# Bucketed attention in front of two MLPs: P's products one step closer to the exponentials, with a new start and one early weight less

## The chip, the cores and the metric

The kernel runs on one core of a Trainium2 chip. The metric is the device time of one execution, in microseconds (us). The engines are TensorE (PE), VectorE (DVE), ScalarE (ACT) and GpSimd (POOL); SyncE (SP) only issues transfers here, and ACT issues some too. All engines take their instructions in the order written.

## What is computed

```python
def reference(**kw):
    # q, k, v: (2, 8, 768, 64), proj: (64, 6)
    mask = bucket(q @ proj > 0)[..., :, None] == bucket(k @ proj > 0)[..., None, :]
    s = where(mask, q @ k.T / 8, -1e9)          # (2, 8, 768, 768)
    p = exp(s - max(s)); p = p / (sum(p) + 1e-9)
    x = (p @ v) as 1536 tokens x 512            # 8 heads side by side
    x = (sigmoid(x @ w_gate) * (x @ w_val)) @ w_out       # 512 -> 1536 -> 512
    h = x @ w_in; return (h * cos(h)) @ w_out2            # 512 -> 2048 -> 512
```

A query sees only the keys whose six projection signs equal its own. The MLP weights come as 64-bit floats.

## The kernel before

Every product is made of high and low float32r parts: a value is rounded to a high part, what is left is the low part, and three (or two) matmuls are added up.

**Attention** (lines 227 to 689) goes through 16 heads of six row blocks of 128 queries, NG = 96 steps in all. Step g issues, among others:

- S, `scores(g+2)` (396): four matmuls of a row block against 768 keys, in one of two double banks `s_ps`. The bucket condition sits in extra rows of the operands (q2, k2);
- MIN, `rowmax(g+1)` (409), one reduction on DVE, and EXP, `expo(g)` (418), one activation with row sums on ACT;
- every third step COEF (433): the reciprocals of three row sums on DVE, and on POOL the coefficient of fully masked rows; NRM (450): P scaled on POOL, one row block (128x768) an instruction;
- the products of P, LAG steps behind: `ptrans` (465) transposes three row blocks of P for one block of 128 keys, `phi` (ACT) and `plo` (DVE) split it, `pv` (485) adds two matmuls with v. Ta, the transposes of the even block, is the first in a step to read a new group of three row blocks 3u, 3u+1, 3u+2, in step 3u + LAG - 1; Tb has the odd one;
- FIN (493): at a block's end ACT copies the output of half a head, which SP's queue puts in place. Three steps after the second head of a pair, `fin_sum` (524) adds the halves on POOL (128x768); five steps after, `fin_hi` (ACT) and `fin_lo` (POOL) write the tokens' high and low parts;
- W, `early_weights` (646): in some steps one of the NEARLY early weights is converted from 64 to 32 bits, in two parts, on ACT and DVE.

The next heads are prepared on the side by PREP: an ordered list `todo` by step. For a head whose first step is s1: loads at s1-19 and s1-17, transposes of its halves at s1-12 and s1-10 (their split, two POOL instructions at lines 300 and 303, comes in LATE of the next step), `bits` (six matmuls, 348) at s1-8, and `values` (v split on POOL, 261) at s1-3 for even, s1-1 for odd heads. `fin_sum` and `fin_lo` are appended to the same lists. The order in a step is written out by hand, from step LAG - 1 on:

```python
ORDER = (
    "Tb LOa COEF NRM PVb EXP Ta MIN LATE W HIb PVa PREP S FIN HIa PVaF LOb".split()
)
```

Before that the fill steps issue only "COEF NRM MIN EXP LATE W PREP S". Heads 0 and 1 are prepared ahead of the first step (599 to 634): head 0's pieces are copied between partitions on DVE, POOL and ACT, head 1's by transfers.

**The two MLPs** (692 to 859) follow in a list of items, each of which is some 12 to 24 matmuls of 512 columns; weights are converted and split some items ahead by due times (824 to 839). The first items run between the last steps of attention.

Of the kernel before, what the change touches and what calls it, by code (L numbers as in the profile page):

```python
# [40 lines left out]
def lsh_attention_glu_moe_cos_moe(  # L41
# [30 lines left out]
    NEARLY, NWE = 3, 5  # L72
# [135 lines left out]
    order = sorted(use, key=lambda kk: use[kk] - lead(kk)[0])  # L208
# [18 lines left out]
    def attention():  # L227
        nonlocal done
        parts = None
        with ExitStack() as st:  # L230
# [40 lines left out]
            def trans(hd, half, fast=False):  # L271
                hh = heads.setdefault(hd, {})
                if half == 0:
                    hh["x"] = [
                        prep.tile([P, T, P], F32R, tag=f"x{i}", name=f"x{i}_{hd}", bufs=2)
                        for i in range(2)
                    ]
                    for nm in ("q1", "k1", "q2", "k2"):
                        hh[nm] = prep.tile([P, T, P], F32R, tag=nm, name=f"{nm}_{hd}")
                xh, xl = hh["x"]  # L280
                sl = slice(3 * half, 3 * half + 3)
                pt = ps_t.tile([P, 3, P], F32, tag="t", name=f"pt{hd}{half}")
# [3 lines left out]
                def evac():  # L286
                    if fast:
                        nc.scalar.activation(xh[:, sl, :], pt, AF.Copy, scale=qscale)
                        nc.vector.scalar_tensor_tensor(
                            out=xl[:, sl, :],  # L290
                            in0=pt,
                            scalar=qscale,
                            in1=xh[:, sl, :].bitcast(F32),
                            op0=ALU.mult,
                            op1=ALU.subtract,
                        )
                    else:
                        xf = work.tile([P, 3, P], F32, tag="xf", name=f"xf{hd}{half}", bufs=2)
                        nc.scalar.activation(xf, pt, AF.Copy, scale=qscale)
                        nc.gpsimd.tensor_scalar(  # L300
                            out=xh[:, sl, :], in0=xf, scalar1=1.0, scalar2=1.0, op0=ALU.mult, op1=ALU.mult
                        )
                        nc.gpsimd.tensor_tensor(
                            out=xl[:, sl, :], in0=xf, in1=xh[:, sl, :].bitcast(F32), op=ALU.subtract
                        )
                    lo, hi = slice(0, D), slice(D, P)
                    if hd == 0:

                        for eng, nm, rows, src, part in (
                            (nc.vector, "q1", hi, xl, lo),  # L310
                            (nc.gpsimd, "q1", lo, xh, lo),
                            (nc.gpsimd, "k1", hi, xh, hi),
                            (nc.gpsimd, "k2", slice(32, 64), xl, slice(64, 96)),
                            (nc.gpsimd, "k2", slice(64, 96), xl, slice(96, 128)),
                        ):
                            eng.tensor_scalar(
                                out=hh[nm][rows, sl],
                                in0=src[part, sl].bitcast(F32),
                                scalar1=1.0,
                                scalar2=1.0,  # L320
                                op0=ALU.mult,
                                op1=ALU.mult,
                            )
                        if half == 1:
                            for nm, rows, part in (
                                ("k1", lo, hi),
                                ("q2", slice(32, 64), slice(0, 32)),
                                ("q2", slice(64, 96), slice(32, 64)),
                            ):
                                nc.scalar.copy(hh[nm][rows], xh[part].bitcast(F32))  # L330
                            raw.pop(hd)
                        return
                    if half == 0:
                        return
                    raw.pop(hd)
                    for nm, rows, src, part in (
                        ("q2", slice(32, 96), xh, lo),
                        ("k2", slice(32, 96), xl, hi),
                        ("q1", hi, xl, lo),
                        ("k1", lo, xh, hi),  # L340
                        ("q1", lo, xh, lo),
                        ("k1", hi, xh, hi),
                    ):
                        nc.sync.dma_start(hh[nm][rows].bitcast(F32), src[part].bitcast(F32))

                return evac

            def bits(hd):
                pb = ps_t.tile([P, HS], F32, tag="t", name=f"pb{hd}")
                hh = heads[hd]  # L350
                xh, xl = hh["x"]
                for half in range(2):
                    sl = slice(3 * half, 3 * half + 3)
                    cols = slice(0, P) if half else slice(D, D + P)
                    for n, (i, x) in enumerate(((0, xh), (1, xh), (0, xl))):
                        nc.tensor.matmul(  # L356
                            pb,
                            pw[:, i, cols],
                            x[:, sl, :],
                            start=(half == 0 and n == 0),  # L360
                            stop=(half == 1 and n == 2),
                        )

                def code(out, rows):
                    nc.vector.tensor_scalar(
                        out=out,
                        in0=pb[rows],
                        scalar1=bcode[rows, 1:2],
                        scalar2=bcode[rows, 0:1],
                        op0=ALU.is_gt,  # L370
                        op1=ALU.mult,
                    )

                def evac():
                    parts = [
                        (half, nm, slice(D * half + 32 * i, D * half + 32 * i + 32))
                        for half, i, nm in ((0, 0, "q2"), (0, 1, "k2"), (1, 1, "k2"), (1, 0, "q2"))
                    ]
                    if hd > 0:
                        bf = prep.tile([P, HS], F32R, tag="bf", name=f"bf{hd}", bufs=1)  # L380
                        code(bf, slice(0, P))
                    for half, nm, rows in parts:
                        out = hh[nm][0:32, 3 * half : 3 * half + 3].rearrange("p t s -> p (t s)")
                        if hd == 0:
                            code(out, rows)
                        else:
                            nc.sync.dma_start(out.bitcast(F32), bf[rows].bitcast(F32))

                return evac
# [159 lines left out]
            LAG = 7  # L549

            WL, WC = (72, 74, 76), 82
# [8 lines left out]
            for hd in range(2, NH):  # L560
                s1 = T * hd
                if hd > 2:
                    for nm in "qk":
                        at(max(s1 + LOAD_AT[nm], -2), lambda hd=hd, nm=nm: load(hd, nm))
                if hd % 2 == 0:
                    at(max(s1 + LOAD_AT["v"], -1), lambda hd=hd: load(hd, "v"))
                for half in range(2):
# [5 lines left out]
                    else:  # L573
                        at(2 * half, lambda hd=hd, half=half: trans(hd, half))
                at(max(s1 + BITS_AT, 2), lambda hd=hd: bits(hd))
# [4 lines left out]
            def run_late():  # L580
                while late:
                    late.pop(0)()
# [7 lines left out]
            with tc.manual_schedule(  # L590
# [14 lines left out]
                for g in range(2):  # L605
                    nc.sync.dma_start(pj[D * g : D * g + D, :], proj)
# [13 lines left out]
                evac = [trans(0, half, fast=True) for half in range(2)]  # L620
                for fn in evac:
                    fn()
                evac = [bits(0)]
                evac += [trans(1, half, fast=True) for half in range(2)]
                for fn in evac:
                    fn()
# [4 lines left out]
                scores(0)  # L631
                scores(1)
                rowmax(0)
                late.append(bits(1))
                for g in range(NG + LAG + 2):
# [22 lines left out]
                    def norms():  # L658
                        for n in range(g - 3, NG if g == NG else g - 2):
# [16 lines left out]
                        "NRM": (0 <= g - 3 <= NG - 3, norms),  # L676
# [15 lines left out]
    def moe():  # L692
        with ExitStack() as st:
# [210 lines left out]
```

## Time and profile before

| | us |
|---|---|
| median of 3 runs | 806.71 (806.35 to 808.7) |
| profiled execution | 806.87 |
| its span, first to last instruction | 805.1 |
| PE busy in the span | 791.7 (98%) |
| DVE busy | 510.2 (63%) |
| ACT busy | 468.0 (58%) |
| POOL busy | 325.6 (40%) |

The shares are means over the attention part, some 250 us in which all four engines work, and the MLPs, in which mostly PE does. Matmuls are pipelined, so their lengths overlap, and a busy PE is not one at its peak.

### The profile page before, as it was taken

To read this page: it belongs to the slowest core of one execution; us is meant where nothing else is said; L and a number is where in the kernel's file an instruction comes from. 1 tells how busy PE (TensorE), PEld (TensorE's weight loads), DVE (VectorE), ACT (ScalarE), POOL (GpSimd) and SP (SyncE) were. 2 spreads that over 40 slices of the span, in tenths; PEclk is the share of its full clock that TensorE was granted. 3 is DMA by queue.
4 is the path that set the end of the run, shared out by engine and by line. 5 is a ranking of instruction groups with operands and counts; after the bars stand their busy time and mean duration, and the time that the engine had idled before them with its cause. 6 is when DMAs were issued, how large, how long until landed. Compare 5 with 4: busy or idle time off the path is not lost.

```text
span 805.1 us, 11607 instructions
## 1 busy us (share of the span) xinstructions
PE 791.7 (98%) x3984; PEld 680.0 (84%) x3984; DVE 510.2 (63%) x794; ACT 468.0 (58%) x929; POOL 325.6 (40%) x347
## 2 busy tenths in 40 slices
PE   7999999999999999999999999999999999999998
PEld 5899999999988888888888888888888888878886
DVE  6888888888985443333343266667655666586662
ACT  5898989989996322222222254456666656564442
POOL 5879889988972212111121122221222122222221
PEclk9999999999999999999999999999999999999999
DMA  6766765688513333222221112323223333242312
GB/s 157 189 156 155 171 163 138 153 196 212 137 47 108 105 105 93 92 78 79 79 78 53 53 55 102 106 79 107 90 91 104 105 105 103 62 161 94 105 53 104
DMA packets 70746, 89.03 MB, mean 111 GB/s; under 512 B 30112, under 2 KB 54816, under 8 KB 70688
## 3 DMA queue, kind: packets, MB, share of 16 engines
q1 hardware_dynamic: 67104, 84.96, 37.2%
q10 hardware_dynamic: 3584, 3.34, 1.5%
q8 instruction: 31, 0.51, 0.3%
q14 instruction: 27, 0.22, 0.1%
HBM read 59.77 MB, written 3.15 MB: 78 GB/s over the span
## 4 chain that ended last, share of the span: by engine, by line
PE 93%; DVE 3%; ACT 2%; issue 1%; DMA 0%; POOL 0%; DVEq 0%; ACTq 0%; POOLq 0%
PE a L807 16%; PE ph L718 16%; PE pv L718 12%; PE a L780 12%; PE pg L718 12%; PE t L470 7%; PE o L491 4%; PE o L490 4%; PE s L403 4%; PE s L406 4%; PE pb L356 2%; PE pt L284 1%; ACT p L421 1%; DVE mn L414 1%; DVE pl L480 0%
## 5 line engine op out<-in xcount | busy, mean ns | idle before, releaser
L718 PE MATMUL ph<-xy,ih 128*128 128x512 f32 x384 | 118.1, 389 | 0.0
L123 ACT CAST gh<-g 128x512 fp32r<-128x512 f32 x84 | 52.1, 620 | 109.8 <-PE a L807 44.5
L480 DVE TENSOR_TENSOR pl<-t,ph 128x384 fp32r<-128x384 f32 x192 | 102.5, 553 | 15.1 <-ACT ph L475 13.5
L124 POOL TENSOR_TENSOR zl<-w_z,zh 128x512 fp32r<-128x512 f32 x32 | 41.4, 1295 | 167.7 <-ACT zh L123 167.7
L454 POOL TENSOR_SCALAR p<-p,r,d 128x768 f32<-128x768 f32 x96 | 95.2, 996 | 21.1 <-PE s L406 7.7
L744 DVE TENSOR_TENSOR g<-pv,sg 128x512 f32<-128x512 f32 x36 | 24.9, 692 | 123.9 <-PE pv L718 122.6
L475 ACT CAST ph<-t 128x384 fp32r<-128x384 f32 x192 | 90.5, 486 | 17.4 <-PE t L470 15.7
L414 DVE TENSOR_REDUCE mn<-s 128x1 f32<-128x770 f32 x96 | 91.2, 951 | 13.6 <-PE s L406 10.6
L470 PE MATMUL t<-ident,p 128*128 128x128 f32 x576 | 94.4, 272 | 0.0
L124 DVE TENSOR_TENSOR gl<-g,gh 128x512 fp32r<-128x512 f32 x84 | 57.8, 688 | 52.7 <-ACT gh L123 50.5
L421 ACT ACTIVATE p<-s,mn 128x768 f32<-128x768 f32 x96 | 88.1, 918 | 5.1 <-DVE mn L414 4.9
L742 ACT ACTIVATE sg<-pg 128x512 f32<-128x512 f32 x36 | 21.3, 592 | 119.4 <-PE pg L718 119.4
L718 PE MATMUL pg<-xy,gh 128*128 128x512 f32 x288 | 89.3, 390 | 0.0
L718 PE MATMUL pv<-xy,vh 128*128 128x512 f32 x288 | 88.7, 389 | 0.0
L718 PEld LDWEIGHTS ph<-xy,ih 128*128 128x128 f32 x384 | 72.0, 188 | 14.9
L470 PEld LDWEIGHTS t<-ident,p 128*128 128x128 f32 x576 | 74.7, 140 | 7.5
L490 PE MATMUL o<-ph,vs 128*128 128x384 f32 x192 | 79.0, 412 | 0.3 <-ACT e L500 0.3
L807 PE MATMUL a<-zh,gh 128*128 128x512 f32 x192 | 74.8, 390 | 0.2 <-DVE o L817 0.2
L807 PE MATMUL a<-zl,gh 128*128 128x512 f32 x192 | 74.8, 390 | 0.2 <-POOL zl L124 0.2
L807 PE MATMUL a<-zh,gl 128*128 128x512 f32 x192 | 74.8, 390 | 0.0
L718 PE MATMUL ph<-xy,il 128*128 128x512 f32 x192 | 74.7, 389 | 0.0
L403 PE MATMUL s<-k,q 96*128 96x384 f32 x192 | 69.7, 363 | 2.1 <-ACT p L421 2.1
(105 smaller groups left out, 1748.3 us busy)
## 6 DMA issues: line engine op xcount, KB each, us to landing
raw_z<-in_moe_w_out SPq DMA_DIRECT2D x32, 512.0 KB, 3.3
raw_o<-in_moe_w_out SPq DMA_DIRECT2D x23, 512.0 KB, 3.3
q<-x SPq DMA_DIRECT2D x45, 192.0 KB, 3.1
k<-x SPq DMA_DIRECT2D x45, 192.0 KB, 3.5
raw_i<-in_moe_w_in SPq DMA_DIRECT2D x16, 512.0 KB, 3.9
raw_v<-in_moe_w_val SPq DMA_DIRECT2D x10, 512.0 KB, 3.5
raw_g<-in_moe_w_gate SPq DMA_DIRECT2D x9, 512.0 KB, 3.7
nv<-in_v SPq DMA_DIRECT2D x8, 384.0 KB, 4.5
```

The lines of the kernel that those rows point to most:

```text
L124: sub.tensor_tensor(out=dst_l, in0=src, in1=dst_h.bitcast(F32), op=ALU.subtract)
L403: nc.tensor.matmul(o, hh["q2"][0:96, t, :], hh["k2"][0:96, sl, :], start=True, stop=False)
L414: nc.vector.tensor_reduce(mn_t[u][:, i : i + 1], s_t[g][:, :, 0 : HS + 1], axis=AX.XY, op=ALU.min)
L421: nc.scalar.activation(pt, s_t.pop(g)[:, :, 0:HS], AF.Exp, bias=mn_t[u][:, i : i + 1], scale=-1.0, accum_out=sm_t[u][:, i : i + 1],)
L454: nc.gpsimd.tensor_scalar(out=pt, in0=pt, scalar1=r[:, i : i + 1], scalar2=d[:, i : i + 1], op0=ALU.mult, op1=ALU.add,)
L470: nc.tensor.transpose(pt[:, i, :], pv_[:, j * P : (j + 1) * P], ident)
L475: nc.scalar.copy(ph, pt_t[w])
L480: nc.vector.tensor_tensor(out=pl, in0=pt_t.pop(w), in1=ph_t[w].bitcast(F32), op=ALU.subtract)
L490: nc.tensor.matmul(o_t[u], vs[:, j, :], ph_t.pop(w), start=(j == 0), stop=False)
L718: nc.tensor.matmul(ps, w[:, kt, :], xy[c][:, hl, kt, :], start=(n == 0), stop=(n == 11))
L780: nc.tensor.matmul(acc[c, e], w[:, e, :], m, start=(f == 0 and n == 0), stop=(f == F1 - 1 and n == 2),)
L807: nc.tensor.matmul(acc[c, t], m[:, ts], w, start=(f == 0 and n == 0), stop=(f == F2 - 1 and n == 2),)
```

## The change

1. LAG goes from 7 to 6. The norms of a group, one in each of the steps 3u+3, 3u+4 and 3u+5, become two in step 3u+3 and one in 3u+4.
2. Two weights instead of three are converted during attention (NEARLY), from step 84 instead of 82; no conversion is made at the MLPs' item 0; the first output weight goes ahead of the second value weight.
3. Head 0 is prepared in an order written by hand (`first_head`): the bits of its two halves go to two banks, k's part and q's first block are coded first. The first scores and the first minimum come ahead of head 1's low parts. Head 1's loads are issued ahead of the bucket constants.
4. Head 2 is split from PSUM by ACT and DVE (as head 1 was) instead of by POOL, one step apart. For every head the high-part matmuls of `bits` come ahead of the low-part ones, and the six transfers that place a head's parts have another order.

```diff
-    NEARLY, NWE = 3, 5
+    NEARLY, NWE = 2, 5
-    order = sorted(use, key=lambda kk: use[kk] - lead(kk)[0])
+    order = sorted(use, key=lambda kk: use[kk] - lead(kk)[0] - 1.5 * (kk == ("o", 0, 0)))
...
+                for low in range(2):
+                    for half in range(2):
+                        for i in range(2 - low):
+                            nc.tensor.matmul(
+                                pb,
+                                pw[:, i, slice(0, P) if half else slice(D, D + P)],
+                                hh["x"][low][:, 3 * half : 3 * half + 3, :],
...
+            def first_head():
+                split = [trans(0, half, fast=True) for half in range(2)]
...
+                pb = [s_ps[1][0:D, 0, 0:HS], ps_o.tile([P, HS], F32, tag="o", name="pb0")[0:D]]
...
+                for high, _ in split:
+                    high()
+                for _, low in split:
+                    low()
                 for half in range(2):
...
+                for ts in (h0, h1):
+                    move(nc.gpsimd, "k1", hi, ts, xh, hi)
+                    for part in (64, 96):
+                        move(nc.gpsimd, "k2", slice(part - 32, part), ts, xl, slice(part, part + 32))
+                move(nc.scalar, "k1", lo, every, xh, hi)
+                move(nc.scalar, "q1", lo, h0, xh, lo)
+                for part in (0, 32):
+                    move(nc.scalar, "q2", slice(part + 32, part + 64), h0, xh, slice(part, part + 32))
+                move(nc.vector, "q1", hi, h0, xl, lo)
+                k_code(0)
+                q_code(0, 0, 1)
+                k_code(1)
+                q_code(0, 1, 3)
+                q_code(1, 0, 3)
+                move(nc.gpsimd, "q1", lo, h1, xh, lo)
+                move(nc.gpsimd, "q1", hi, h1, xl, lo)
...
-            LAG = 7
+            LAG = 6
-            WL, WC = (72, 74, 76), 82
+            WL, WC = (72, 74, 76), 84
...
-                        at(max(s1 + LOAD_AT[nm], -2), lambda hd=hd, nm=nm: load(hd, nm))
+                        at(max(s1 + LOAD_AT[nm], -2) if hd > 3 else 2, lambda hd=hd, nm=nm: load(hd, nm))
...
-                at(max(s1 + BITS_AT, 2), lambda hd=hd: bits(hd))
+                at(s1 + BITS_AT if hd > 2 else 5, lambda hd=hd: bits(hd))
...
-                    nc.sync.dma_start(pj[D * g : D * g + D, :], proj)
+                    (nc.sync, nc.scalar)[g].dma_start(pj[D * g : D * g + D, :], proj)
+                load(1, "k")
+                load(1, "q")
                 for g in range(2):
                     nc.sync.dma_start(
                         bcode[D * g : D * g + D],
...
-                load(1, "q")
-                load(1, "k")
-                load(0, "v")
                 load(2, "k")
                 load(2, "q")
+                load(0, "v")
                 bit_weights()
...
+                rest = first_head()
+                split = [trans(1, half, fast=True) for half in range(2)]
+                for high, _ in split:
+                    high()
+                place(1, 0)
+                rest()
+                scores(0)
+                scores(1)
+                rowmax(0)
...
+                late.append(first_low)
+                at(1, lambda: bits(1)())
                 values(0)
                 values(1)
...
-                        for n in range(g - 3, NG if g == NG else g - 2):
+                        for n in {0: range(g - 3, NG if g == NG else g - 1), 1: (g - 2,), 2: ()}[g % 3]:
                             norm(n)
...
-                        "NRM": (0 <= g - 3 <= NG - 3, norms),
+                        "NRM": (3 <= g <= NG, norms),
...
-                    convert_at[k] = max(early, k - NEARLY, split_at[order[k - NWE]] if k >= NWE else 0)
+                    convert_at[k] = max(early, k - NEARLY, 1, split_at[order[k - NWE]] if k >= NWE else 0)
```

## Rows read from the trace of the kernel before

**Rows 1.** The page, busy time and share of each engine
```profile
PE 791.7 (98%) x3984; PEld 680.0 (84%) x3984; DVE 510.2 (63%) x794; ACT 468.0 (58%) x929; POOL 325.6 (40%) x347
```

**Rows 2.** Windows: stretch, length, busy us (instructions) by engine, clock, DMA share
```profile
3.80:13.60 9.80, 8.96 (x29) 7.31 (x30) 8.23 (x16) 5.38 (x8) 7.04 (x12) 1.00 0.62 147
16.20:17.60 1.40, 0.29 (x4) 0.06 (x2) 1.17 (x2) 1.03 (x3) 1.22 (x2) 1.00 1.00 232
17.60:24.30 6.70, 5.44 (x29) 4.38 (x29) 4.14 (x7) 4.93 (x12) 4.93 (x7) 1.00 0.87 195
60.00:200.00 140.00, 140.00 (x941) 133.00 (x941) 121.06 (x205) 128.63 (x306) 125.01 (x153) 1.00 0.69 168
```

**Rows 3.** Timeline of PE, steps 46 to 48; start us, length us, engine, operation
```profile
117.73 1.29 PE L356 MATMUL pb<-x,pw 128*128 128x384 f32 x6
...
120.59 0.49 PE L470 MATMUL t<-ident,p 128*128 128x128 f32 x3
...
122.66 0.61 PE L470 MATMUL t<-ident,p 128*128 128x128 f32 x3
```

**Rows 4.** Timeline of POOL, steps 45 to 47
```profile
114.99 0.98 POOL L454 TENSOR_SCALAR p<-p,r,d 128x768 f32<-128x768 f32 x1 [1.10 <-PE s L406]
115.95 0.51 POOL L300 TENSOR_SCALAR x<-xf 128x384 fp32r<-128x384 f32 x1
...
117.53 0.50 POOL L265 TENSOR_SCALAR vs<-nv 128x384 fp32r<-128x384 f32 x1
...
119.11 0.99 POOL L454 TENSOR_SCALAR p<-p,r,d 128x768 f32<-128x768 f32 x1
120.06 1.85 POOL L527 TENSOR_TENSOR ef<-e,ef 128x768 f32<-128x768 f32 x1
121.88 1.00 POOL L454 TENSOR_SCALAR p<-p,r,d 128x768 f32<-128x768 f32 x1
```

**Rows 5.** Timelines of ACT and DVE, steps 43 and 45
```profile
111.21 0.49 ACT L500 COPY e<-o 128x384 f32<-128x384 f32 x1
...
114.63 0.17 DVE L447 RECIPROCAL r<-sm 128x3 f32<-128x3 f32 x1
```

**Rows 6.** Line 527, the sum: nanoseconds least, median, most; first and last start
```profile
L527 POOL TENSOR_TENSOR ef<-e,ef x8: 1017/1836/1851, 62.9 to 246.4; 128x768 f32<-128x768 f32 x7, 128x384 f32<-128x384 f32 x1
```

**Rows 7.** Timelines of POOL and PE, steps 10 and 11
```profile
34.00 1.95 POOL L454 TENSOR_SCALAR p<-p,r,d 128x768 f32<-128x768 f32 x2
...
35.14 0.49 PE L470 MATMUL t<-ident,p 128*128 128x128 f32 x3
```

**Rows 8.** Timelines of DVE and POOL, step 83
```profile
207.14 1.22 DVE L160 SCALAR_TENSOR_TENSOR w_g<-wp_g,wl_g 128x512 int32<-128x512 int32 x1
...
207.80 1.41 POOL L454 TENSOR_SCALAR p<-p,r,d 128x768 f32<-128x768 f32 x1
```

**Rows 9.** Timelines of SyncE's queue, DVE, ACT and PE, the start
```profile
4.91 0.65 SPq L256 DMA_DIRECT2D nqk<-in_k  x1
...
8.19 0.66 DVE L365 TENSOR_SCALAR q<-pb,bcode 32x384 fp32r<-32x384 f32 x1 [0.26 <-PE pb L356]
...
10.99 1.14 DVE L289 SCALAR_TENSOR_TENSOR x<-pt,qscale,x 128x384 fp32r<-128x384 f32 x2
...
13.03 0.90 ACT L421 ACTIVATE p<-s,mn 128x768 f32<-128x768 f32 x1 [1.97 <-DVE mn L414]
...
22.74 0.49 PE L470 MATMUL t<-ident,p 128*128 128x128 f32 x3
```

**Rows 10.** Timelines of DVE and PE, the tail of attention
```profile
239.13 1.51 DVE L155 TENSOR_SCALAR wl_v<-raw_v 128x512 int32<-128x512 int32 x1
...
241.15 0.44 PE L491 MATMUL o<-pl,vs 128*128 128x384 f32 x1 [1.04 <-DVE pl L480]
```

**Rows 11.** Timeline of PE, the same kind of matmul early and later
```profile
11.84 0.52 PE L406 MATMUL s<-k,q 128*128 128x384 f32 x1
...
17.86 0.34 PE L406 MATMUL s<-k,q 128*128 128x384 f32 x1
```

More of the change, by code (lines that the diff above doesn't have):

```diff
@@ L284, in trans @@
                     nc.tensor.transpose(pt[:, i, :], raw[hd][:, 3 * half + i, :], ident)
[L286 to L334, printed above, removed]
-                    raw.pop(hd)
[L336 to L344, printed above, removed]
@@ new lines, in trans, with place @@
+                return (high, low) if fast else both
+            def place(hd, i):
+                lo, hi = slice(0, D), slice(D, P)
+                if i == 0:
+                    raw.pop(hd)
+                hh = heads[hd]
+                for nm, rows, part in (
+                    (("q2", slice(32, 96), lo), ("k1", lo, hi), ("q1", lo, lo), ("k1", hi, hi)),
+                    (("k2", slice(32, 96), hi), ("q1", hi, lo)),
+                )[i]:
+                    nc.sync.dma_start(hh[nm][rows].bitcast(F32), hh["x"][i][part].bitcast(F32))
@@ L348, in bits, with code @@
+            def code(out, pb, rows):
+                nc.vector.tensor_scalar(
+                    out=out,
+                    in0=pb,
+                    scalar1=bcode[rows, 1:2],
+                    scalar2=bcode[rows, 0:1],
+                    op0=ALU.is_gt,
+                    op1=ALU.mult,
+                )
             def bits(hd):
@@ new lines, in evac, with send @@
+                def evac():
+                    bf = prep.tile([P, HS], F32R, tag="bf", name=f"bf{hd}", bufs=1)
+                    code(bf, pb, slice(0, P))
+                    def send(half, i, eng=nc.sync):
+                        rows = slice(D * half + 32 * i, D * half + 32 * i + 32)
+                        out = hh["qk"[i] + "2"][0:32, 3 * half : 3 * half + 3].rearrange("p t s -> p (t s)")
+                        eng.dma_start(out.bitcast(F32), bf[rows].bitcast(F32))
+                    send(0, 0)
+                    send(0, 1)
+                    if hd == 1:
+                        late.append(lambda: send(1, 1, nc.scalar))
+                    else:
+                        send(1, 1)
+                    send(1, 0)
@@ L352, in bits @@
                 for half in range(2):
-                    sl = slice(3 * half, 3 * half + 3)
-                    cols = slice(0, P) if half else slice(D, D + P)
-                    for n, (i, x) in enumerate(((0, xh), (1, xh), (0, xl))):
+                    for n, (i, low) in enumerate(((0, 0), (1, 0), (0, 1))):
                         nc.tensor.matmul(
[L357 to L361, printed above, removed]
-                        )
@@ L364, in code @@
[L364 to L387, printed above, removed]
@@ L389, in bits @@
-                return evac
+                            pb[half],
+                            pw[:, i, D : 2 * D],
+                            hh["x"][low][:, 3 * half : 3 * half + 3, :],
+                            start=(n == 0),
+                            stop=(n == 2),
+                        )
+                for ts in (h0, h1):
+                    move(nc.gpsimd, "k1", hi, ts, xh, hi)
+                    for part in (64, 96):
+                        move(nc.gpsimd, "k2", slice(part - 32, part), ts, xl, slice(part, part + 32))
@@ L391, in attention, with rest @@
+                move(nc.gpsimd, "q1", hi, h1, xl, lo)
+                def rest():
+                    for part in (0, 32):
+                        move(nc.scalar, "q2", slice(part + 32, part + 64), h1, xh, slice(part, part + 32))
+                return rest
             s_t, p_t, mn_t, sm_t, ra_t, o_t, e_t, f_t = ({} for _ in range(8))
@@ L580, in run_late, with second_head, lower, upper @@
             def run_late():
-                while late:
-                    late.pop(0)()
+                now = late[:]
+                late.clear()
+                for fn in now:
+                    fn()
+            def second_head(half):
+                high, low = trans(2, half, fast=True)
+                def lower():
+                    low()
+                    if half == 1:
+                        place(2, 0)
+                        place(2, 1)
+                def upper():
+                    high()
+                    late.append(lower)
+                return upper
             def run_todo(step):
@@ L613, in attention, with first_low @@
                     )
-                load(1, "q")
-                load(1, "k")
-                load(0, "v")
                 load(2, "k")
                 load(2, "q")
+                load(0, "v")
                 bit_weights()
[L620 to L626, printed above, removed]
+                rest = first_head()
+                split = [trans(1, half, fast=True) for half in range(2)]
+                for high, _ in split:
+                    high()
+                place(1, 0)
[3 more added lines that the diff above has]
+                rowmax(0)
+                def first_low():
+                    for _, low in split:
+                        low()
+                    place(1, 1)
+                late.append(first_low)
+                at(1, lambda: bits(1)())
                 values(0)
@@ L630, in attention @@
                 run_todo(-1)
[L631 to L634, printed above, removed]
                 for g in range(NG + LAG + 2):
```

56 lines of the change are left out of this document (54 added, 2 removed).

## The prediction

> **What bounds the kernel now.** I read the engine table first: TensorE (PE) is busy 98% of a span of 805.1 us [rows 1]. Busy matmuls overlap, so I then cut the span into windows [rows 2]. From 60 to 200 us, the middle of attention, PE has 140.00 us of 140.00: no gap anywhere. Only the start has holes: of 1.40 us from 16.20 PE works 0.29, of 6.70 us from 17.60 it works 5.44. So the work on PE, which this change leaves as it is (the same matmuls, in another order), sets the time; a microsecond is won only where PE stands idle, and a microsecond for which PE newly waits is added whole, since nothing later has slack to give it back.
>
> The third view is PE against GpSimd (POOL) in one period of attention [rows 3, 4]. A step g makes one row block of scores, and steps repeat in a period of twelve (two heads). The transposes named Ta of step 47 are at 120.59, those of step 48 at 122.66, one step or 2.07 us later. In step 48 Ta is the first reader of rows 42 to 44 of P, normalised. Those three transposes need 0.61 us instead of 0.49: the last one waits. The timeline of POOL shows for what. Its normalisation of row 44 starts at 121.88 and ends at 122.88, 0.2 us after that group of transposes has begun. So POOL, 89% busy here (125.01 of 140.00 us [rows 2]), already comes out exactly at its due time.
>
> **The change part by part.**
>
> *LAG 7 to 6, and the norms.* P's products of step g now belong to a block one step younger: the first Ta on rows 3u to 3u+2 moves from step 3u+6 to 3u+5. The norms of these rows ran in steps 3u+3, 3u+4, 3u+5; now two run in 3u+3 and the third in 3u+4. POOL takes its instructions in the order written, so I write that order out for the period above (u = 14, coefficients in step 45). Before: norm 42 at 114.99, the split of a head's transposed half at 115.95, the values of the next head at 117.53, norm 43 at 119.11, the sum `fin_sum` at 120.06, norm 44 at 121.88 [rows 4]. After: `fin_sum` hangs on the finish of a head, which LAG moves one step up, from step 46 to 45; split and values stay in step 45. The new order is norm 42, norm 43, split, values, sum, norm 44. The same six pieces, 7.89 us from 114.99, and norm 44 again last: 122.88. But its reader is now Ta of step 47: 120.59, the third transpose two spacings of 0.11 later, 120.81. The third transpose is 2.07 us late, one step.
>
> What could shorten it: the chain starts 0.36 us after the reciprocal at 114.63 [rows 5], POOL having waited 1.10 us for it [rows 4]. The copy of a finished output on ScalarE (ACT), 0.49 us [rows 5], leaves step 43 for steps 42 and 45, so exponential 44 and with it the reciprocal may come earlier; at most by that copy, at least by nothing. I take 0.22, since the reciprocal is also queued behind two subtractions of P on VectorE (DVE): 1.85 us a period, bounds 1.58 and 2.07.
>
> How often: the sum over 128x768 occurs 7 times from 62.9 us on [rows 6]; split and values lie beside it in steps 21, 33, 45, 57, 69 and 81, six times; at the seventh, step 93, the last heads are already prepared. 6 x 1.85 = **11.1**. In step 9 all but the sum is there: norms end at 34.00 + 1.95 = 35.95, and Ta of step 11 begins at 35.14, third transpose 35.36 [rows 7]: 0.6 late, 0.4 with the same 0.22: **+0.4**. The small wait in Ta of steps 24, 36, ... 84 goes: 0.12 by the row (0.61 less 0.49), of which I count 0.07, since PE resumes without losing the rest: **-0.4** for six. The other three groups in a period fit: their third norm has no sum ahead of it. `fin_lo`, now in step 47, runs behind norm 44 and ahead of the coefficients of step 48, in the time in which PE waits.
>
> Of the six third norms that of step 83 took 1.41 us [rows 8], against 1.00 of the others, as in [rows 4]. It ran beside a weight conversion on DVE [rows 8], which WC = 84 moves two steps later. I therefore use the plain length for all six; with the long one the sixth stall is 0.43 longer. The Trainium skill (GPSIMD Engine Reference, section 1, Specifications) says that POOL's SBUF interfaces are shared with VectorE and contend when DVE reads two SBUF inputs, which a conversion's second half does; the rows agree. By that rule the 0.43 goes, as in my sum; without it the sixth stall is 2.3.
>
> *The split's late end.* In step 46 the bit matmuls start at 117.73 [rows 3]; their last needs the low part of the split. One norm more ahead of it in the queue puts that part's end from 117.53 to about 118.5; the new order takes the low parts last in a group which starts at 117.73 + 1.29 - 0.34 = 118.7 (the last one's own 0.34 as in [rows 11]). I take nothing; bounds 0 and 0.3, seven times.
>
> *The start.* Now the first row minimum stands on DVE behind four codes from 8.19 and two low parts of head 1, 1.14 us from 10.99 [rows 9]. After the change head 0's bits go into two banks, so that codes start when the first three matmuls are through and DVE has done its copy: three matmuls of 0.52 [rows 11] are 1.56 at most, I take half, about 7.4. The codes, 10.99 - 8.19 = 2.8 and 0.1 for cutting one in two, then end at 10.3; the scores, which also need POOL's copies, at about 10.6, the minimum a good 0.9 later (12.13 to 13.03). The first exponential, 13.03 [rows 9], moves to about 11.6: 1.4 us. PE passes head 1's transposes on the way, so their loads count too: issued behind the bucket constants, at 4.91 the last [rows 9], they go ahead of those, some 2 us earlier. Moved along: the projection's second load goes from SyncE's queue to ACT's, ahead of ACT's table load; head 0's v goes behind head 2's loads; head 3's loads go to step 2; one code transfer of head 1 is issued by ACT in step 2. An issue holds a queue 0.65 us [rows 9]; what waits behind them (table, values) is not due for 2 us or more, except that ACT issue, which holds exponential 3 up to 0.65. And the first transposes of P (22.74 [rows 9], step 6) come in step 5, so one step of product work, about 1.0 us, fills PE where it now idles. Against it, four low parts on DVE in the fill (2.3 us, of which some 0.6 on the chain). 1.4 + 1.0 - 0.6 = **-1.8**; bounds 0 (the codes' copies land late, or the clock below) and -3.5 (the 1.11 + 1.26 us idle of [rows 2] and 1.4 together, less what must remain).
>
> *Two early weights.* A third conversion leaves attention, and none is made at the first item of the MoE. In the tail DVE works 1.51 us on a conversion from 239.13 and PE waits 1.04 us for the subtraction behind it [rows 10]: **-1.0**, bounds 0 (another piece may land there) and -1.0. The one that leaves attention: between 0 and the same 1.04, I take **-0.5**. The two then lie in items of 5 us on PE where DVE is half idle: nothing. The order of the output weight against the value weight: nothing either, both are due items later; if that cover were gone, one DVE piece, 1.5.
>
> *The tail.* `fin_lo` of the last but one pair moves from step 99 to 95, ahead of the last three norms: 0 to 1.0 of PE waiting, I take **+0.5**.
>
> Sum: 11.1 + 0.4 - 0.4 - 1.8 - 1.0 - 0.5 + 0.5 = +8.3. The profiled execution took 806.87 us (span 805.1 plus 1.8 around it), 0.16 above the median of 806.71: **815.1 us** from either, to 0.2.
>
> **The rivals.**
>
> *The chain on POOL fits after all* (faster). Then only the other terms are left: 806.87 - 1.8 - 1.0 - 0.5 - 0.4 + 0.5, 803.7. It decides at one place: norm 42 would have to start by 112.9 on the clock of [rows 4], 2.07 earlier; POOL has 1.10 us idle ahead of it, which speaks for something, but exponential 44 and its row sum come only just before the reciprocal. 0.11.
>
> *The sum is not in that queue*, because the finish does not move or something slips behind norm 44. Then each period is like step 9: 0.4 x 7 instead of 11.5, 806.87 + 2.8 - 3.2 = 806.5: within 0.3%, which is 2.4 us and about what a measurement of this kernel can tell from no change. 0.08.
>
> *The clock falls after each stall* (slower still). The same 128x384 matmul takes 0.52 us at 11.84 and 0.34 at 17.86 [rows 11]; the first is the lower of the two levels (1.2 and 2.4 GHz), though the granted clock stands at 1.00 in both windows [rows 2]. Against it: 17.86 comes just after PE stood still for 1.1 us and is at the higher level. If a stall of 1.85 us brought the low level for one step of 2.07 us, it would cost 2.07 x 0.53 = 1.1, seven times: 822.8. 0.04. The Trainium skill (TensorE: Matmul & The Clock Gate, Part 1) says that the throttled state is the default and that activity releases it, so idle time speaks against this change; by that rule taken strictly this rival would be the forecast, and the row at 17.86 is why it isn't.
>
> **How the numbers follow.** My forecast has 0.77, the rivals 0.11, 0.08 and 0.04. Its own bounds: stalls 9.5 to 12.9, start 0 to -3.5, the rest -2.0 to +2.5; together rarely below 809 or above 819. The range 808 to 819.5 leaves out the fast rival, most of the second, and the clock. Slower by over 0.3%: 0.80 (forecast and clock, less 0.01 for a forecast that comes out small); within: 0.09; faster: 0.11.
>
> **What would show it.** In the timeline of POOL: norm, norm, split, values, sum, norm in steps 21, 33, ... 81; PE idle about 1.9 us before the third transpose there, released by POOL's norm, six times, some 30.5 us apart; a window of 60 to 200 us with some 130 of 140 us busy. First exponential near 11.6, first transposes of P near 20.5; no wait of 1 us in the tail. Wrong if the middle of attention stays at 100% busy, if the sum lands behind the third norm, or if the spacing of matmuls doubles after a stall.

## The result, and the profile after

The changed kernel takes 818.88 us (median of 4, 817.86 to 819.34) against 807.15 of the kernel before: ratio 1.0144, 95% interval 1.0129 to 1.016. It is 11.7 us slower; 815.1 was forecast, with 808.0 to 819.5 as the range.

First the page of the changed kernel: its span, the busy times, and the chain that ended last by engine.

```profile
span 817.5 us, 11623 instructions
...
PE 793.2 (97%) x3984; PEld 681.9 (83%) x3984; DVE 511.4 (63%) x796; ACT 472.4 (58%) x932; POOL 321.6 (39%) x343
...
PE 85%; POOL 7%; DVE 3%; DMA 2%; ACT 1%; issue 1%; SPq 0%; POOLq 0%; DVEq 0%; ACTq 0%
```

PE's work is the same (793.2 against 791.7 busy, [rows 1]), and so is the number of matmuls; the span has grown by 12.4. POOL now has 7% of the chain, where the page of the kernel before gave it 0%:

```profile
PE 93%; DVE 3%; ACT 2%; issue 1%; DMA 0%; POOL 0%; DVEq 0%; ACTq 0%; POOLq 0%
```

The windows (columns as in [rows 2]) say where the time goes:

```profile
17.60:24.30 6.70, 5.56 (x34) 4.70 (x33) 5.53 (x9) 5.39 (x13) 4.94 (x6) 1.00 0.95 228
60.00:200.00 140.00, 130.91 (x861) 125.35 (x860) 111.59 (x188) 120.08 (x280) 115.19 (x141) 0.98 0.64 152
...
65.40:69.90 4.50, 4.36 (x20) 4.17 (x21) 2.48 (x5) 3.24 (x8) 4.31 (x7) 0.63 0.54 126
69.90:95.00 25.10, 25.10 (x171) 24.29 (x170) 20.70 (x36) 22.43 (x53) 18.77 (x25) 1.00 0.57 136
```

From 60 to 200 us PE now works 130.91 of 140.00, where it had 140.00 before [rows 2]. And there is something that I had given 0.04: in the 4.50 us from 65.40 the granted clock is 0.63 of full speed; from 69.90 it is back at 1.00.

The timeline of POOL in the same steps 45 to 47 as [rows 4]:

```profile
119.95 1.97 POOL L502 TENSOR_SCALAR p<-p,r,d 128x768 f32<-128x768 f32 x2 [1.28 <-DVE r L495]
121.88 0.51 POOL L302 TENSOR_SCALAR x<-xf 128x384 fp32r<-128x384 f32 x1
122.48 1.02 POOL L305 TENSOR_TENSOR x<-xf,x 128x384 fp32r<-128x384 f32 x1
123.47 0.52 POOL L265 TENSOR_SCALAR vs<-nv 128x384 fp32r<-128x384 f32 x1
124.07 1.01 POOL L268 TENSOR_TENSOR vs<-nv,vs 128x384 fp32r<-128x384 f32 x1
125.04 1.81 POOL L575 TENSOR_TENSOR ef<-e,ef 128x768 f32<-128x768 f32 x1
126.84 0.99 POOL L502 TENSOR_SCALAR p<-p,r,d 128x768 f32<-128x768 f32 x1
```

Two norms, the split (two instructions), the values (two), the sum, the third norm: the order that the prediction wrote out, 7.87 us from 119.95 to 127.82 (7.89 before). And PE in step 47:

```profile
125.68 0.38 PE L518 MATMUL t<-ident,p 128*128 128x128 f32 x2
127.88 0.36 PE L518 MATMUL t<-ident,p 128*128 128x128 f32 x1 [1.82 <-POOL p L502]
127.96 0.60 PE L538 MATMUL o<-ph,vs 128*128 128x384 f32 x1
128.36 0.52 PE L539 MATMUL o<-pl,vs 128*128 128x384 f32 x1
128.68 0.52 PE L451 MATMUL s<-k,q 96*128 96x384 f32 x1
```

Two transposes of Ta run at 125.68, the third waits 1.82 us for POOL's norm. Measured by start to start, 1.98 us are lost here; the same occurs at 63.45, 95.39, 157.68, 188.07 and 218.39, 1.98 to 2.02 us each, 11.9 in sum. After this one the matmuls of 128x384 take 0.52 instead of 0.34 and start 0.32 us apart instead of 0.177: the lower of the two clock levels, as in [rows 11]. That follows on two of the six stalls, at 63.45 and 125.79. By the excess of spacing up to the return of the higher level they cost 1.5 and 1.4 us.

At the start (before: 13.03 and 22.74, [rows 9]) the first exponential and the first transposes of P stand here:

```profile
10.94 0.90 ACT L469 ACTIVATE p<-s,mn 128x768 f32<-128x768 f32 x1 [0.34 <-DVE mn L462]
...
19.12 0.75 PE L518 MATMUL t<-ident,p 128*128 128x128 f32 x3
```

What the start gained is read where the scores of row block 12 begin, in this kernel (first line) and in the one before (second):

```profile
33.32 0.34 PE L451 MATMUL s<-k,q 96*128 96x384 f32 x1
...
33.41 0.34 PE L403 MATMUL s<-k,q 96*128 96x384 f32 x1
```

They begin 0.1 us earlier, and with LAG 6 PE has by then done six transposes of P and six matmuls with v more. In the trace of the kernel with LAG 7 below, such work takes 1.37 us (24.70 to 26.07, six transposes and four matmuls) and 0.35 (31.94 to 32.29, two matmuls), so that the start gained about 1.8 by this estimate. The tail of attention (timelines of DVE, PE and POOL):

```profile
244.75 1.60 DVE L124 TENSOR_TENSOR gl<-w_g,gh 128x512 fp32r<-128x512 f32 x1
...
246.87 0.44 PE L539 MATMUL o<-pl,vs 128*128 128x384 f32 x1 [1.21 <-DVE pl L528]
...
248.43 1.98 POOL L595 TENSOR_TENSOR xy<-ef,xy 128x256 fp32r<-128x256 f32 x2
...
253.81 0.33 PE L518 MATMUL t<-ident,p 128*128 128x128 f32 x1 [0.64 <-POOL p L502]
```

The conversion of [rows 10] is gone, but a weight's split of 1.60 us on DVE lies in its place, and PE waits 1.21 behind it instead of 1.04. Later `fin_lo`, 1.98 us on POOL ahead of the last norms, costs another 0.64. The tail is 0.6 us longer than before.

Account of the span: six stalls 11.9, clock 2.9, start -1.8, tail 0.6, step 11 0.2: 13.8. Against the measured 12.4 that leaves -1.4. The weights' part ahead of the tail is some -0.5 of it (by the run with the weights alone, below); the rest, many waits under 0.15 us, was not taken apart.

### The profile page after: what moved, and what is told of

The parts are those of the page before. It is cut to its first block, busy times and chain, and to the rows that moved or that the text cites. A ratio compares the mean times of both kernels' runs of the same rounds, so it can differ in the third digit from the quotient of the medians.

```text
span 817.5 us, 11623 instructions
## 1 busy us (share of the span) xinstructions
PE 793.2 (97%) x3984; PEld 681.9 (83%) x3984; DVE 511.4 (63%) x796; ACT 472.4 (58%) x932; POOL 321.6 (39%) x343
## 4 chain that ended last, share of the span: by engine, by line
PE 85%; POOL 7%; DVE 3%; DMA 2%; ACT 1%; issue 1%; SPq 0%; POOLq 0%; DVEq 0%; ACTq 0%
PE a L878 15%; PE ph L789 15%; PE pv L789 12%; PE a L851 12%; PE pg L789 12%; PE t L518 5%; PE s L451 3%; PE s L454 3%; POOL p L502 3%; PE o L539 3%; PE o L538 3%; POOL ef L575 2%; DMA nqk<-in_q 1%; PE pb L342 1%; POOL vs L268 1%; PE pt L284 1%
## 5 line engine op out<-in xcount | busy, mean ns | idle before, releaser
L518 PE MATMUL t<-ident,p 128*128 128x128 f32 x576 | 97.1, 275 | 11.7 <-POOL p L502 11.6
L523 ACT CAST ph<-t 128x384 fp32r<-128x384 f32 x192 | 92.3, 485 | 25.3 <-PE t L518 23.1
```

Source lines behind the costliest of these rows:

```text
L518: nc.tensor.transpose(pt[:, i, :], pv_[:, j * P : (j + 1) * P], ident)
L523: nc.scalar.copy(ph, pt_t[w])
```

## The experiments

The theory: one queue on POOL, in which the third norm stands behind split, values and sum, makes the stalls, and a stall now and then lets the clock fall. The rival: LAG 6 is too short in itself, so that a wait removed turns up at the next link. All medians in us, with the ratio to the kernel before on the same chip. Beside these runs the kernel before read 806.23 to 806.64, and 807.15 beside the changed kernel; so differences between two kernels of different rows, or from the changed kernel's 818.88, hold to about 1 us.

| kernel | median | ratio, 95% interval |
|---|---|---|
| sum later | 816.52 | 1.0126 (1.0112 to 1.0140) |
| LAG 7, new start, two weights | 802.85 | 0.9959 (0.9947 to 0.9972) |
| before, with LAG 6 and new norms alone | 821.69 | 1.0192 (1.0178 to 1.0206) |
| stalls filled with PE work | 815.92 | 1.0120 (1.0104 to 1.0135) |
| sum and writes later | 807.51 | 1.0013 (1.0004 to 1.0022) |
| the same, and values earlier | 833.69 | 1.0328 (1.0305 to 1.0350) |
| LAG 6, one norm a step | 824.34 | 1.0221 (1.0208 to 1.0234) |
| before, with two weights alone | 804.67 | 0.9979 (0.9970 to 0.9987) |
| values later | 808.58 | 1.0025 (1.0016 to 1.0034) |
| values, sum and writes later | 805.66 | 0.9990 (0.9981 to 0.9999) |
| LAG 7 as above, sum and writes later | 804.43 | 0.9976 (0.9967 to 0.9985) |

**Sum later.**

```diff
-SUM_AT, HIGH_AT, LOW_AT = 3, 5, 5
+SUM_AT, HIGH_AT, LOW_AT = 4, 5, 5
```

> The changed kernel with the sum of a pair of heads one step later (fin_sum four steps behind the finish instead of three), so that on GpSimd the third norm of its group comes ahead of the sum. Queue theory (the six stalls of 2 us are the third norm waiting behind split, values and sum in one queue): the norm ends 1.8 us earlier, six stalls of 0.1 to 0.4 instead of 1.98, no fall of the clock behind them, 803.5 to 806. Rival, lag (with P's products one step younger the way from the exponential over the reciprocal to the transposes is too short in itself): the wait goes to another link, stalls of over 1 us stay, 813 to 818. Rival, clock only (the low level after a stall is most of the loss): as the queue theory here, so the next kernels tell them apart.

816.52: a miss, and inside the range given to the rival. Timelines of POOL, ACT and PE in steps 34 to 36:

```profile
92.87 0.98 POOL L502 TENSOR_SCALAR p<-p,r,d 128x768 f32<-128x768 f32 x1
93.82 1.84 POOL L575 TENSOR_TENSOR ef<-e,ef 128x768 f32<-128x768 f32 x1
...
95.69 0.93 ACT L591 CAST xy<-ef 128x512 fp32r<-128x512 f32 x2 [1.88 <-POOL ef L575]
...
97.64 0.55 PE L284 MATMUL pt<-ident,nqk 128*128 128x128 f32 x3 [1.33 <-DVE pl L528]
```

The third norm now comes ahead of the sum, and the stall in Ta falls to 0.2 us, as the queue theory has it. But the sum ends at 95.66, and ACT stands in front of `fin_hi` for it, 1.88 us; the high part of Ta's block is queued behind, and PE waits 1.33 (1.5 by spacing). One piece moved, the next reader in the chain was another engine's queue. So far the rival could claim this run too.

**LAG 7 with the new start and two weights.**

```diff
-            LAG = 6
+            LAG = 7
-                        for n in {0: range(g - 3, NG if g == NG else g - 1), 1: (g - 2,), 2: ()}[g % 3]:
+                        for n in range(g - 3, NG if g == NG else g - 2):
-                        "NRM": (3 <= g <= NG, norms),
+                        "NRM": (0 <= g - 3 <= NG - 3, norms),
```

> The changed kernel with LAG 7 and one norm a step as before: the new start and the two early weights alone. Both theories: no stall of 1.98 us in the middle of attention, 100% busy there. The start is worth about 1.0 (first exponential near 10.9 as in the changed kernel, but the product work again one step later), the weights and the tail 0 to 1.5: 804.5 to 806.5, 0.1 to 0.3% under the kernel before. If the start or the weights held part of the loss, it would be over 807.

802.85, faster than expected, and faster than both kernels. Its window of the middle, and where the scores of row block 12 begin on PE:

```profile
60.00:200.00 140.00, 140.00 (x942) 132.93 (x942) 121.32 (x206) 128.68 (x305) 124.56 (x152) 1.00 0.69 168
...
31.23 0.34 PE L451 MATMUL s<-k,q 96*128 96x384 f32 x1
```

140.00 of 140.00 again. So the loss lies wholly in LAG and norms, and the rest of the change gains 0.41%, 3.4 us. The scores begin 2.2 us earlier than in the kernel before (33.41), with the same work ahead of them: that is the start's part.

**LAG 6 and the norms alone.** The mirror image, in the kernel before: the same lines the other way round.

> The kernel before with LAG 6 and the new norms alone, its start and its three early weights kept. Queue theory: six stalls of about 2 us, low clock behind some of them, gain of one step at the start about 1.0: 818 to 822, so 1 to 3 us above the changed kernel. Rival (the new start, with its other phase of the queues, makes the stalls): near 807.

821.69, as expected: six stalls of 1.98 us or more, and the low clock after two of them. The third transpose of step 47, and POOL's norm and the third transpose at the sixth stall:

```profile
130.54 0.38 PE L470 MATMUL t<-ident,p 128*128 128x128 f32 x1 [1.82 <-POOL p L454]
...
222.34 1.41 POOL L454 TENSOR_SCALAR p<-p,r,d 128x768 f32<-128x768 f32 x1
...
223.81 0.33 PE L470 MATMUL t<-ident,p 128*128 128x128 f32 x1 [2.46 <-POOL p L454]
```

The weight conversion on DVE keeps its place here, and its second half lies beside the sixth third norm (222.02, 0.88 us). That norm is long again, 1.41 us as in [rows 8], and PE waits 2.46 for it instead of 1.82.

**Stalls filled.** In `ptrans`, ahead of the third transpose of the first block, for u = 6, 10, ... 26:

```diff
+                    if i == 2 and j == 0 and u >= 6 and u % 4 == 2 and u < 30:
+                        p0 = p_t[3 * u].rearrange("p a s -> p (a s)")
+                        for _ in range(14):
+                            nc.tensor.transpose(pt[:, 0, :], p0[:, 0:P], ident)
```

> The changed kernel with 14 more transposes of the first row block, written over the same place with the same values, between the second and the third transpose of Ta in steps 23, 35, 47, 59, 71 and 83, that is inside the six stalls: 14 x 0.108 = 1.5 us of PE work where PE stood still for 1.8. Queue theory with a clock term of its own (idle time in a stall lets the clock fall now and then, some 2 us a time): the stalls stay, PE's idle time in them falls to 0.3, the granted clock stays at 1.00 behind all six, 814.5 to 816.5. Rival (the low clock has nothing to do with idle time): the dips stay, 818 to 820. If the work did not fit into the stall: up to 9 us more.

815.92, as expected, although PE has 9 us more to do: 3.0 us under the changed kernel, or 2.0 when each is set against the kernel before that ran beside it. Timeline of PE in step 35:

```profile
93.75 1.69 PE L521 MATMUL t<-ident,p 128*128 128x128 f32 x14
95.72 0.33 PE L522 MATMUL t<-ident,p 128*128 128x128 f32 x1 [0.28 <-POOL p L502]
...
96.41 0.34 PE L454 MATMUL s<-k,q 128*128 128x384 f32 x1
```

The 14 transposes take 1.69 us of the stall, PE waits 0.28, and the next matmuls run at 0.34. None of the six stalls is followed by the low level. So the clock's part is real, 2 to 3 us, and here it goes when PE is not idle in the stall; a stall that is filled costs its 2 us alone. The granted clock of whole executions agrees: 0.996, 0.996, 0.998 and 0.996 in the four runs of the changed kernel, 0.999 to 1.000 in the four of this one. But long stalls are not the only occasion: of the runs with LAG 7 above, which has none, one of five read 0.998 and took 804.16 us.

**One norm a step with LAG 6.** The norm lines of the diff above, LAG left at 6.

> The changed kernel (LAG 6) with its norms one a step as before, the third in the step in which it is read. Queue theory: the third norm is last in the same six pieces either way, so the six stalls stay at about 2 us; the other groups lose up to 0.4 us each where a split now stands between the norms: 818 to 823. Rival (it is the pairing of two norms in one step that makes the third late): the stalls go, 803 to 808.

824.34, a little over the range. Timelines of POOL and PE, steps 33 to 35:

```profile
92.51 0.52 POOL L265 TENSOR_SCALAR vs<-nv 128x384 fp32r<-128x384 f32 x1
...
94.08 1.84 POOL L575 TENSOR_TENSOR ef<-e,ef 128x768 f32<-128x768 f32 x1
95.91 1.94 POOL L502 TENSOR_SCALAR p<-p,r,d 128x768 f32<-128x768 f32 x2
...
96.95 0.33 PE L518 MATMUL t<-ident,p 128*128 128x128 f32 x1 [0.99 <-POOL p L502]
97.91 0.33 PE L518 MATMUL t<-ident,p 128*128 128x128 f32 x1 [0.64 <-POOL p L502]
```

The queue now has one norm ahead of split, values and sum, and two behind. Two transposes wait, 0.99 and 0.64 us, for the same sum of work. The pairing of two norms is no cause of the loss; it takes 5.5 us off what LAG 6 costs with the old norms. The low level follows here too, behind the second and the sixth of the six pairs of waits; the window behind the second:

```profile
97.90:102.40 4.50, 4.49 (x21) 4.36 (x22) 2.64 (x5) 3.57 (x8) 4.10 (x5) 0.66 0.41 98
```

**Values later.** The even heads' v is split in step 10 of 12.

```diff
-VALUES_AT = (-3, -1)
+VALUES_AT = (-2, -1)
```

> The changed kernel with the values of the even heads one step later (step 10 of 12 instead of 9), so behind the third norm; the sum stays ahead of it. Queue theory: the chain of split, sum and norm is shorter by the values' 1.6 us, the six stalls shrink from 1.98 to about 0.4, too short for the clock to fall: 805.5 to 808. Rival (one late piece is as bad as another, the stall is a whole step whatever the queue holds): 815 or more.

808.58: 10.3 us off the loss with one number changed. Timelines of POOL and PE, steps 45 to 47:

```profile
119.52 1.84 POOL L575 TENSOR_TENSOR ef<-e,ef 128x768 f32<-128x768 f32 x1
121.36 0.97 POOL L502 TENSOR_SCALAR p<-p,r,d 128x768 f32<-128x768 f32 x1
...
122.38 0.33 PE L518 MATMUL t<-ident,p 128*128 128x128 f32 x1 [0.27 <-POOL p L502]
```

The norm comes straight behind the sum; PE waits 0.27, that is 0.40 to 0.43 by spacing against 1.98 (once 0.97, in step 35). A piece of 1.6 us out of the queue, 1.57 out of the stall, and the clock at 1.00 throughout. This is the dose that the queue theory asked for; that a late norm costs a whole step whatever stands ahead of it is out. The median lies 0.6 over the range, since 0.26 is lost in a later Ta of each period.

**Sum and writes later.** As the first experiment, with `HIGH_AT, LOW_AT = 6, 6`.

> The changed kernel with the sum four steps behind the finish instead of three, and the writes of the tokens' high and low parts (fin_hi on ScalarE, fin_lo on GpSimd) six instead of five; in the run with the sum alone moved, ScalarE stood 1.9 us in front of fin_hi for the late sum and PE lost 1.5 us behind it. Queue theory: neither the third norm nor fin_hi is late, stalls of 0.2 us at most, no fall of the clock, 802.5 to 804.5, the kernel before or better. Rival, lag (LAG 6 is too short, the wait only moves from link to link): a third place shows a stall of over 1 us in each period, 812 to 818.

807.51: no stall over 1 us is left, 11.4 us of the loss are gone; but 3 us more than expected stay. In each period PE loses 0.2 us three times. One of them, on ACT and DVE:

```profile
94.80 0.93 ACT L591 CAST xy<-ef 128x512 fp32r<-128x512 f32 x2
95.63 0.48 ACT L548 COPY e<-o 128x384 f32<-128x384 f32 x1
...
96.52 0.56 DVE L528 TENSOR_TENSOR pl<-t,ph 128x384 fp32r<-128x384 f32 x1 [0.84 <-ACT ph L523]
```

`fin_hi` now falls into the step in which ACT also copies a finished output; the high part behind both comes late, and DVE waits 0.84 for it.

**The same, and values earlier** (`VALUES_AT = (-4, -1)`).

> As the run beside it, and the values of the even heads one step earlier (step 8 of 12, in which GpSimd has no norm). Queue theory: the third norm comes 1.6 us earlier still, the 0.2 us goes too: 801.5 to 804, as good as LAG 7 with the new start (802.85) or up to 1 us better, since the first products come a step earlier. If LAG 6 gains nothing at the start, the same as LAG 7 within 0.5 us. If the v load is late for the values: a wait on GpSimd of up to 1 us in each period, of which PE sees little.

833.69, the worst of all. The queue of SP, and POOL:

```profile
93.65 0.59 SPq L249 DMA_DIRECT2D nv<-in_v  x1
...
98.93 0.51 POOL L265 TENSOR_SCALAR vs<-nv 128x384 fp32r<-128x384 f32 x1 [3.58 <-DMA nv<-in_v]
```

The load of v is issued at 93.65, and the values, which now come before the data have landed, stop POOL for 3.58 us. Behind them stand the norms and the split, and PE's bit matmuls wait 1.6 to 3.1 us for it (start to start) in six periods. The low level follows on five of these waits (granted clock 0.50 to 0.70 over the next 4.50 us), so the 833.69 are not the waits alone. I had named the late load and priced it at nearly nothing for PE: the wrong half of the same theory, since everything behind a waiting instruction waits too.

**Values, sum and writes later** (`VALUES_AT = (-2, -1)`, `SUM_AT, HIGH_AT, LOW_AT = 4, 7, 8`).

> The changed kernel (LAG 6) with the values of the even heads in step 10, the sum four, fin_hi seven and fin_lo eight steps behind the finish: the third norm has neither values nor sum ahead of it, and fin_hi is no longer in a step with a finish's copy, where in the run with six and six ScalarE was late by 0.2 us. Queue theory: no wait over 0.15 us left in the middle of attention, 802 to 804, as LAG 7 with the new start and weights (802.85); if the earlier products gain at the start, down to 801.5. Rival, lag: LAG 6 costs some 4 us in small waits wherever the pieces lie, 806 to 808.

805.66, between the two ranges, and the window of the middle:

```profile
60.00:200.00 140.00, 139.86 (x930) 131.75 (x928) 117.53 (x204) 126.92 (x299) 123.42 (x151) 1.00 0.70 167
```

LAG 6 without its stalls: 13.2 us under the changed kernel, 1.0 under the one before on the same chip, but 2.8 over LAG 7 (on the medians of two sets of runs). Of the waits over 0.15 us one is left ahead of the conversions, 0.29 at 187 us; so are a dozen of 0.10 to 0.13. So the rival holds a small part: 2 to 3 us. Some 0.4 of it lies in the start (as in the changed kernel, below); which link makes the rest wasn't taken apart.

**Two weights alone.** The lines NEARLY, order, WC and `convert_at` of the diff, in the kernel before.

> The kernel before with the two early weights alone (NEARLY 2, from step 84, none at item 0, the output weight ahead). My prediction gave them 1.5 us: 804.7. If the whole 3.4 us of LAG 7 with start and weights came from the start, it would be 806.2; from the accounts of PE's waits the tail gives 1.2 and the start 2.1, so 805.0 is expected.

804.67, 1.8 under the kernel before. The tail loses 1.3 us less in its profile.

**LAG 7, sum and writes later** (`4, 6, 6` in the kernel with LAG 7 above).

> LAG 7 with one norm a step, the new start and the two weights (802.85), and the sum four, the writes six steps behind the finish: the third norm in step 11 comes ahead of the sum, so the 0.1 us that PE still loses six times should go: 802.0 to 802.9, hardly to be told from 802.85. If ScalarE's fin_hi collides with a finish's copy, up to 1.5 more.

804.43: the 0.1 us became 0.59 in each period, by PE's spacing ahead of a product with v. Timelines of ACT and PE there:

```profile
94.77 0.93 ACT L591 CAST xy<-ef 128x512 fp32r<-128x512 f32 x2
95.60 0.48 ACT L548 COPY e<-o 128x384 f32<-128x384 f32 x1
...
96.13 0.44 PE L538 MATMUL o<-ph,vs 128*128 128x384 f32 x1 [0.43 <-ACT e L548]
```

With the writes six steps behind, `fin_hi` falls into the step of the finish's copy, as in the run above, and PE waits 0.43 for ACT: the collision that the expectation had priced at up to 1.5. The kernel with LAG 7 alone stays the best.

## Why the prediction was right

- *Norms and LAG.* 11.1 forecast for six stalls of 1.85, measured 11.9 for six of 1.98. The order of the queue, its 7.9 us and the six steps came as written. The correction by an earlier reciprocal was too large: from reciprocal to the third transpose PE now has 6.32 us (119.58 to 125.90, had it not waited), before 6.18; 0.14 instead of 0.22. Step 11: 0.2 instead of 0.4. That the stall is the sum of the pieces ahead of the norm is shown by two runs that take out one piece each, the sum (0.2 us left in Ta) and the values (0.40 to 0.43 left, once 0.97).
- *Three other terms.* The split's late end cost nothing. The long norm did not come back: its rows of POOL show 0.98 to 0.99 us for the third norms of all six stalls, with the conversion moved. Where the conversion stayed (the kernel before with LAG 6 alone) the sixth took 1.41, 0.43 more as priced, and the stall was 0.64 longer. The Trainium skill (GPSIMD Engine Reference, section 1, Specifications) says that POOL's SBUF interfaces are shared with VectorE and contend with a DVE instruction of two SBUF inputs; both traces agree.
- *The start.* -1.8 forecast, about -1.8 measured, but not by its parts: luck. The first exponential came at 10.94 instead of 11.6, and the hand-written start alone gave 2.2 in the kernel with LAG 7. That the products begin a step earlier, priced at -1.0, gave nothing and took back 0.4: with LAG 6 these scores begin 2.1 us later, for 1.7 us of product work. Near 23 us PE waits 0.63 us for DVE there, with LAG 7 0.28. The step moved work forward and filled no gap.
- *Weights and tail.* -1.5 and +0.5 forecast, +0.6 measured in the tail. Alone, the weights gave 1.8, so their size was right; with LAG 6 another piece, the weight's split, lay on DVE in the conversion's place. That was the bound of 0, not my value. The wait of 1.21 us there is also against the prediction's own sign, no wait of 1 us in the tail.
- *The clock.* The term that failed. I set all or nothing against each other, seven falls at 0.04 (where my own count has six stalls), and took none. Two of six stalls were followed by the low level; they cost 1.5 and 1.4 us, where 1.1 was priced, and the filled kernel gives 2 to 3 back. My own sign of being wrong, a spacing of matmuls that doubles after a stall, showed behind these two (0.32 instead of 0.177). The row at 17.86 showed that one gap of 1.1 us left the clock up, and I took it for the rule; 1.8 us of idle time decide otherwise now and then. The Trainium skill (TensorE: Matmul & The Clock Gate, Part 1) says that the throttled state is the default and that activity releases it; taken strictly, as in the prediction, that fits two of the six stalls and not the other four.
- *The size.* The clock's 2.9 us are most of the 3.8 between 815.1 and 818.9; the other misses, stalls 0.8 longer in sum and a tail that gained nothing, were nearly made up by what the account leaves open (-1.4). That 818.88 lies in a range that left the clock out is in part luck: with a fall behind each of the six stalls (6 x 1.45 instead of 2.9, an estimate) it would have been near 825.

The rival in which the chain fits after all is out, and so is that of the sum in another place; what decided it is the order written in the queue.

## What to carry to other kernels

Before a reader is moved a step up, write out the queue of the engine that feeds it, with everything else that lands in those steps, and compare its end with the reader's new time; where the end is already at the due time (here a third transpose that waited 0.1 us), a step earlier costs nearly a step each time (1.98 of 2.07 us). A piece moved out of the way has a reader of its own, and a piece moved too early waits for its data with all that is queued behind it: move consumer and producer together, and look at the data's landing time first. A stall of a saturated TensorE costs more than its length when the clock falls behind it (1.4 to 1.5 us more here).

## What the runs showed of the hardware that I had not expected

Standing idle for 1.82 us in the middle of dense work was followed by the lower clock level in two stalls of six, the first and the third, in the changed kernel and likewise in the kernel before with LAG 6 alone; the window of 4.50 us behind one of them has a granted clock of 0.63. With 1.69 us of transposes in the same gaps the level stayed up behind all six.

The other traces show that the length of the wait alone does not decide. Two waits of about 0.98 and 0.64 us within a microsecond (LAG 6, one norm a step) were followed by the low level in two cases of six. Five waits of 1.33 us (sum later) were followed by none, nor was one of 2.46 (the kernel before with LAG 6), while all five of 2.4 to 2.9 us with values earlier were. What sets the stalls with a fall apart from those without wasn't found.

At the start the granted clock reads 1.00 [rows 2] while the spacing is that of the lower level (0.32 us between matmuls of 128x384, 0.177 later), so there the spacing of equal matmuls tells more than the clock's column.
